# Batch 0's v in two halves around the token weights, its causal masks ahead of the scores, and batch 1's masks on GpSimd

## The chip, the cores and the metric

The kernel runs on one core of one Trainium2 chip. The metric is the device time of one execution in microseconds (us); the time before is the median of 5 runs. Engine names in the text: PE is TensorE (its weight loads, PEld, overlap it), DVE is VectorE, ACT is ScalarE, POOL is GpSimd, SP is SyncE, whose queue (SPq) issues the DMAs. L613 is line 613 of the kernel before.

## The reference

```
q, k, v: (8 batches, 8 heads, 576, 64)   s: (8, 8, 576)
scores = q @ k^T / 8;  cum = cumsum(max(s, 0))
scores = where(j > i, -1e9, scores + min(-(cum_i - cum_j), 0))
x = softmax(scores) @ v                  -> (8, 576, 512), the heads side by side
u = x + (relu(x^T @ w_tok1) @ w_tok2)^T  # w_tok1 576x256, w_tok2 256x576
out = u + relu(u @ w_ch1) @ w_ch2        # w_ch1 512x1536, w_ch2 1536x512
```

All inputs and the output are float32.

## The kernel before

Each batch goes through four stages. **Attention** works on four heads at a time (a "quad", heads 0 to 3 and 4 to 7). k and q of a quad come as one load each (L640), are cast to bf16 in two halves (L659 on POOL, L661 on DVE, L663 on ACT) and are rearranged by a DVE transpose (L670). The scores (L703) are computed in two phases, each into four PSUM banks of 128x512, keys on the partitions and a band of queries on the columns: only key blocks near the diagonal are kept. ACT takes their exponential into the tile E (L719). The decay of the reference is not added to the scores; it is put as a factor exp(cum_j − half) on row j of v and on a column of ones beside it, so the sum that divides comes out of the same product. The table wT of these factors comes from s (L567 to L586). Each 128-row chunk of v is loaded for all eight heads (L613, rows of 256 B) and multiplied by wT (L620) into the tile vp. The value product (L744, nine matmuls a head), a reciprocal (L753) and a normalisation (L758) give x.

The causal mask of the 128x128 diagonal blocks is made in one of two ways. In batches below PMASK, which is 2, TensorE adds it: after a phase's scores a matmul of the identity with the tile neg (0 or −30000) accumulates into the same banks (L712). In later batches POOL zeroes the upper triangle of E after the exponential (L727, one instruction for a key block of all four heads).

**Token mixing** multiplies x by w_tok1 and w_tok2. Batch 0 does it in four column blocks m so that it can begin with two heads (L864 first product, L871 relu, L877 transpose of x added in, L883 second product, L889 copy into uTa). Batch 1 and later do it for all columns (L969, L977, L994, L998), add x on DVE (L1011), and turn the result round by TensorE (L1024, L1032, batch 1) or by DMA. **Channel mixing** is L906 and L929 for batch 0 and L1052 and L1078 for the others. The weights are loaded in float32 into buffers that are used for other things later (uTb and x for the token weights, ga and vf for the channel weights), and cast to bf16 (L787 POOL, L789 DVE, L791 ACT). w_ch1 and w_ch2 come in four quarters each (L829, L837).

**The order is planned.** Each piece of work is put into a list with the engines that may run it, its costs on them, what it reads and writes, and a priority; `Plan.run` simulates the list several times, keeps the shortest plan, and the instructions are emitted in the order of the start times in it. Each engine then runs its own instructions in that order. The `lead` of an item is added to its urgency. The loads (`load_op`) are chained, so SP issues them in the order of the list. Rings of buffers (`Ring`, `Buf`) are handed out in the plan too; the PSUM rings are psc and pmx, four banks each. In the first 45 us of the plan, free PE time is filled with products of zeros (L1191). The loads of the start are listed as follows, which is the order of the SP queue:

```
stage_qk(0, 0); stage_s(); stage_qk(0, HQ); stage_v(0)
load_tok1; load_tok2; load_ch1 x4
stage_qk(1, 0); load_ch2(.., 0); stage_qk(1, HQ); load_ch2(.., 1); load_ch2(.., 2)
stage_v(1); load_ch2(.., 3); then batches 2 to 7
```

Of the kernel before, what the change touches and what calls it, by code (L numbers as in the profile page):

```python
# [49 lines left out]
class Plan:  # L50
# [101 lines left out]
    def run(self, passes=6):  # L152
# [3 lines left out]
        for i in range(passes):  # L156
            self.reset()
            if i >= 5:
                for o in self.ops:
                    o.tail = o.base + (rng.gauss(0.0, 2.0) if rng.random() < 0.1 else 0.0)  # L160
            order, length = self.once(i > 0)
            if best is None or length < best[0]:
                best = (length, [(o, o.start, o.fin, o.eng, o.fn) for o in order],
                        [(b, b.slot, b.begin, b.end) for o in order for b in o.bufs],
                        {r: list(r.uses) for o in order for b in o.bufs for r in (b.ring,)})
            self.lengths.append(round(length, 1))
            if i < 5 or best[0] == length:
                self.tails(order)
                for o in self.ops:
                    o.base = o.tail  # L170
# [9 lines left out]
    def once(self, use, eps=0.03):  # L180
# [14 lines left out]
        port = 0.0  # L195
        order = []

        def slot_time(o):
            t = 0.0
            want = {}  # L200
            for b in o.bufs:
                if b.slot is None:
                    r = b.ring
                    if b.ordered and r.queue[0] is not b:
# [237 lines left out]
def kernel(  # L442
# [28 lines left out]
    PMASK = 2  # L471
    HQ = 4
    TP = 128 // HQ
# [19 lines left out]
    neg = sb("neg", [128, 128], BF16, fast)  # L493
# [67 lines left out]
    def act(n, fn, bias=False):  # L561
# [3 lines left out]
        lambda: nc.sync.dma_start(out=s_sb[:, :], in_=s.rearrange("b h s -> (b h) s")), ["s"], 1.0)  # L565

    def decay():  # L567
        P.op(act(576, lambda: nc.scalar.activation(out=s_sb[:, :], in_=s_sb[:, :], func=AF.Relu)),
             reads=["s"], writes=["sr"], prio=-1)
        P.op({"DVE": (1.3, 1.6, lambda: nc.vector.tensor_tensor_scan(  # L570
            out=cum[:, :], data0=one_sb[:, :].to_broadcast([64, S]), data1=s_sb[:, :], initial=0.0, op0=ALU.mult, op1=ALU.add))},
            reads=["sr"], writes=["cum"], prio=-1)
        P.op(dve(1, lambda: nc.vector.tensor_scalar(
            out=half[:, :], in0=cum[:, S - 1 : S], scalar1=-0.5, scalar2=None, op0=ALU.mult)),
            reads=["cum"], writes=["half"], prio=-1)
        P.op(act(576, lambda: nc.scalar.activation(
            out=wn[:, 0:S], in_=cum[:, :], func=AF.Exp, bias=half[:, 0:1], scale=1.0), True),
            reads=["half", "cum"], writes=["wn"], prio=-1, lead=12.0)
        bw = Buf(r_sc, False)

        def w_tr():
# [6 lines left out]
            reads=[(bw, 0)], writes=["wT"], prio=-1)  # L588
# [11 lines left out]
    nc.vector.memset(ones[:, :], 1.0)  # L600

# [4 lines left out]
    def stage_v(b):  # L606
        vf, vp = Buf(r_vf), Buf(r_vp[b % 2])
        vbuf[b] = vp
        for c in range(NJ):
            n = min(128, S - c * 128)  # L610

            def load(c=c, n=n):
                nc.sync.dma_start(out=vf.t[0:n, c, :, :],  # L613
                                  in_=v[b, :, c * 128 : c * 128 + n, :].rearrange("h p d -> p h d"))
            load_op(load, [(vf, c)], 1.22 * n / 128)
        for c in range(NJ):
            n = min(128, S - c * 128)

            def mul(eng, c=c, n=n):
                eng.tensor_tensor(  # L620
# [619 lines left out]
```

## Time and profile before

| what | value |
|---|---|
| runs | 295.03 us median of 5 (294.57 to 297.26) |
| the profiled execution | 295.55 us, of which the span from first to last instruction is 293.7 us |
| PE busy | 279.3 us, 95% of the span |
| DVE, ACT, POOL busy | 171.5, 182.3, 93.5 us |
| DMA packets | 68050, 54.09 MB, mean 184 GB/s |
| L703 scores, L744 value product | 20.1 us and 18.4 us of PE |
| L712 masks by PE, both batches | 80 matmuls, from 9.6 to 48.2 us |
| L727 masks by POOL | 60 instructions, 36.1 us |

Busy time is how long an engine had an instruction in work; PE's ends are modelled, and the products of zeros count. A stage of the span is read by the engines' busy time in it, and what an engine waits for by the instruction that released it.

### The profile page before, as it was taken

How to read it: one execution, taken by the hardware profiler on the slowest of the kernel's cores; microseconds unless marked ns; L12 is line 12 of the kernel's file. 1: busy time of each engine (PE TensorE's matmuls, PEld its weight loads, DVE VectorE, ACT ScalarE, POOL GpSimd, SP SyncE). 2: the span in 40 equal slices, each digit the busy share in tenths (PEclk: the TensorE clock that was granted, in tenths of full speed). 3: DMA queues.
4: the chain of work that ended last, by engine and by line, in shares of the span. 5: the costliest groups of instructions: out<-in, count | busy, mean ns of one | idle time of the engine just before them, and what ended most of it. 6: DMA issues, size and time to landing. Idle time of an engine off the chain costs nothing.

```text
span 293.7 us, 6606 instructions
## 1 busy us (share of the span) xinstructions
PE 279.3 (95%) x2565; PEld 156.1 (53%) x2597; DVE 171.5 (58%) x332; ACT 182.3 (62%) x344; POOL 93.5 (32%) x138
## 2 busy tenths in 40 slices
PE   8899998969899989999999999999999999999994
PEld 2575455536664534546754545456754545347643
DVE  4883874987977625696847748596425523540022
ACT  3866865779897847965986178866882255007600
POOL 3443200858918412731481113821211210000000
PEclk9999999999999999999999999999999999999999
DMA  7999999998479999988493755567002420150023
GB/s 238 270 326 356 400 273 310 218 358 222 156 216 260 279 226 355 216 187 281 111 214 72 213 209 210 197 152 163 2 0 56 125 74 0 56 143 37 3 71 112
DMA packets 68050, 54.09 MB, mean 184 GB/s; under 512 B 53680, under 2 KB 56560, under 8 KB 68016
## 3 DMA queue, kind: packets, MB, share of 16 engines
q1 hardware_dynamic: 68016, 53.64, 64.8%
q8 instruction: 21, 0.34, 0.5%
q14 instruction: 13, 0.11, 0.1%
HBM read 40.65 MB, written 9.44 MB: 171 GB/s over the span
## 4 chain that ended last, share of the span: by engine, by line
PE 69%; DMA 12%; SPq 8%; DVE 4%; ACT 4%; issue 2%; POOL 1%; DVEq 0%; ACTq 0%
PE pmx L1052 27%; PE pmx L1078 22%; SPq L613 7%; DMA ga<-in_moe_w_ch_dram 4%; PE pmx L744 4%; PE psc L703 4%; PE pmx L994 4%; PE pmx L969 4%; DMA qkf<-in_q_dram 2%; DMA qkf<-in_k_dram 2%; DMA vf<-in_v_dram 2%; ACT E L719 1%; PE pmx L929 1%; ACT junk L645 1%; DMA uTa<-ua 1%
## 5 line engine op out<-in xcount | busy, mean ns | idle before, releaser
L719 ACT ACTIVATE E<-psc 128x512 bf16<-128x512 f32 x120 | 62.9, 603 | 20.9 <-PE psc L703 13.2
L1052 PEld LDWEIGHTS <-wc 128*128 128x128 bf16 x528 | 50.5, 98 | 35.5 <-issue 5.4
L727 POOL TENSOR_SCALAR_AFFINE_SELECT E<-E 128x512 bf16<-128x512 bf16 (+1 forms) x60 | 36.1, 631 | 86.9 <-ACT E L719 70.1
L1052 PE MATMUL pmx<-uTb,wc 128*128 128x320 bf16 x384 | 54.4, 299 | 2.5 <-ACT uTb L1032 1.7
L1078 PE MATMUL pmx<-wc,gb 128*128 128x512 bf16 (+1 forms) x245 | 53.2, 369 | 0.5 <-issue 0.2
L1058 ACT ACTIVATE gb<-pmx 128x320 bf16<-128x320 f32 x79 | 34.3, 439 | 24.3 <-PE pmx L1052 17.7
L645 ACT ACTIVATE junk<-qkf 128x1152 bf16<-128x1152 f32 x32 | 37.3, 1165 | 14.3 <-DMA qkf<-in_k_dram 9.4
L1078 PEld LDWEIGHTS <-gb 128*128 128x128 bf16 x252 | 23.8, 98 | 25.4 <-issue 0.7
L1052 PE MATMUL pmx<-uTa,wc 128*128 128x512 bf16 x137 | 32.4, 379 | 1.4 <-DMA uTa<-ua 1.0
L620 POOL TENSOR_TENSOR vp<-vf,wT 128x512 bf16<-128x512 f32 (+1 forms) x30 | 30.6, 1044 | 9.6 <-PE pmx L744 9.3
L1078 PE MATMUL pmx<-wc,ga 128*128 128x512 bf16 x138 | 32.6, 379 | 0.4 <-issue 0.2
L659 POOL CAST qkb<-qkf 128x1152 bf16<-128x1152 f32 (+1 forms) x15 | 15.7, 1045 | 38.4 <-DMA qkf<-in_q_dram 14.7
L758 DVE TENSOR_TENSOR x<-pmx,rc 128x320 bf16<-128x320 f32 x52 | 25.5, 490 | 1.7
L744 PEld LDWEIGHTS <-E 128*128 128x128 bf16 x576 | 20.9, 97 | 6.0 <-issue 0.9
L1058 ACT ACTIVATE ga<-pmx 128x512 bf16<-128x512 f32 x24 | 14.4, 599 | 15.0 <-PE pmx L1052 14.9
L670 DVE STREAM_TRANSPOSE kT<-qkb 128x576 f32<-128x576 f32 x16 | 20.1, 1255 | 5.7 <-PE psc L703 4.1
L1086 DVE TENSOR_TENSOR of<-pmx,ub 128x512 f32<-128x512 f32 (+1 forms) x17 | 11.2, 658 | 18.3 <-PE pmx L1078 14.5
L1078 PEld LDWEIGHTS <-ga 128*128 128x128 bf16 x144 | 13.3, 98 | 15.6 <-issue 1.1
L670 DVE STREAM_TRANSPOSE qT<-qkb 128x576 f32<-128x576 f32 x16 | 20.0, 1250 | 2.4 <-POOL qkb L659 1.1
L703 PE MATMUL psc<-qT,kT 32*128 32x256 bf16 (+2 forms) x592 | 20.1, 251 | 1.1 <-ACT E L719 0.4
L703 PEld LDWEIGHTS <-kT 32*128 32x128 bf16 x640 | 13.6, 92 | 11.3 <-issue 9.4
L744 PE MATMUL pmx<-vp,E 128*128 128x65 bf16 x468 | 18.4, 193 | 0.0
(107 smaller groups left out, 285.5 us busy)
## 6 DMA issues: line engine op xcount, KB each, us to landing
qkf<-in_k_dram SPq DMA_DIRECT2D x20, 576.0 KB, 6.0
qkf<-in_q_dram SPq DMA_DIRECT2D x20, 576.0 KB, 6.1
vf<-in_v_dram SPq DMA_DIRECT2D x32, 256.0 KB, 6.0
out_dram<-of SPq DMA_DIRECT2D x31, 256.0 KB, 2.6
ga<-in_moe_w_ch_dram SPq DMA_DIRECT2D x6, 768.0 KB, 7.5
vf<-in_moe_w_ch_dram SPq DMA_DIRECT2D x2, 768.0 KB, 9.8
out_dram<-of SPq DMA_DIRECT2D x10, 128.0 KB, 2.7
vf<-in_v_dram SPq DMA_DIRECT2D x8, 128.0 KB, 5.2
```

The lines of the kernel that those rows point to most:

```text
L613: nc.sync.dma_start(out=vf.t[0:n, c, :, :], in_=v[b, :, c * 128 : c * 128 + n, :].rearrange("h p d -> p h d"))
L620: eng.tensor_tensor(out=vp.t[0:n, c, :, 0:D], in0=vf.t[0:n, c, :, :], in1=wT[0:n, c, b * H : b * H + H].unsqueeze(2).to_broadcast([n, H, D ...
L645: P.op({"ACT": (1.1, 1.5, lambda: nc.scalar.activation(out=junk[:, :], in_=f.t[:, :], func=AF.Square, accum_out=sq[:, col : col + 1]))}, r ...
L670: nc.vector.transpose(out=T.t[:, 0:S, :].rearrange("p s q -> p (s q)").bitcast(FP32).rearrange("p (t r) -> p r t", r=R), in_=t1.t[:, :].bi ...
L703: nc.tensor.matmul(out=ps[e].t[:, c0 : c0 + z - a], lhsT=kT.t[p0 : p0 + TP, jc * 128 : jc * 128 + 128, qq], rhs=qT.t[p0 : p0 + TP, a:z, qq ...
L719: nc.scalar.activation(out=E.t[:, e, ph * 512 : ph * 512 + 512], in_=p.t[:, :], func=AF.Exp, scale=0.125)
L727: nc.gpsimd.affine_select(out=w, in_=w, compare_op=ALU.is_ge, fill=0.0, base=0, pattern=[[0, HQ], [1, n]], channel_multiplier=-1)
L744: nc.tensor.matmul(out=o[:, ic, 0 : D + 1], lhsT=E.t[:, hh, d0 : d0 + 128], rhs=vp.t[:, jc, h + hh, 0 : D + 1], start=(jc == j_lo), stop=( ...
L758: nc.vector.tensor_tensor(out=x.t[:, :, (h + hh) * D : (h + hh + 1) * D], in0=o[:, :, 0:D], in1=rc.t[:, :].unsqueeze(2).to_broadcast([128, ...
L1052: nc.tensor.matmul(out=pm.t[:, 0 : e - a], lhsT=wc1[:, m, cc * 128 : cc * 128 + 128], rhs=uT.t[:, m, a:e], start=(m == 0), stop=(m == NMC ...
L1058: lambda cc=cc, pm=pm, a=a, e=e: nc.scalar.activation(out=g.t[:, cc, a:e], in_=pm.t[:, 0 : e - a], func=AF.Relu),
L1078: nc.tensor.matmul(out=pm.t[:, na:nb], lhsT=g.t[:, cc, c * 128 : c * 128 + 128], rhs=wc2[:, cc, na:nb], start=(cc == 0), stop=(cc == NCC - 1))
```

## The change

- v of batch 0 is loaded and scaled in two parts of four heads. The first part stays where v was; the second is listed behind both token weights, with the second quad behind it. Of the first part's five chunks the first three (c up to VP = 2) are scaled by POOL only; the rest of batch 0's may go to POOL or DVE.
- PMASK goes from 2 to 1: batch 1 is masked by POOL on E.
- In batch 0 the mask product comes ahead of the scores of its phase, as an item of its own that needs only the tile neg. neg is now 256 wide, the right half zero, so the mask product writes the whole width of each key block and opens the accumulation; the scores close it.
- The casts of batch 0's k and q have a fixed engine each. The token weights' casts may go to POOL or ACT (only POOL before), and w_tok2 is cast in two pieces.
- The list of loads has k and q of batch 1's second quad ahead of the first quarter of w_ch2.
- Planner: batch 0's items get large leads; costs of some loads differ; batch 0's score and value banks are handed out in a listed order; `run` does 5 plain passes and 60 more with small random changes of urgency around the best so far (one such pass before).

The diff, cut to its core:

```diff
-    def run(self, passes=6):
+    def run(self, passes=5, search=60):
...
-            if i >= 5:
+            if i >= passes:
                 for o in self.ops:
-                    o.tail = o.base + (rng.gauss(0.0, 2.0) if rng.random() < 0.1 else 0.0)
+                    o.tail = base[o] + (rng.gauss(0.0, 2.0) if rng.random() < 0.02 else 0.0)
...
-    PMASK = 2
+    PMASK = 1
     HQ = 4
+    VP = 2
...
-    neg = sb("neg", [128, 128], BF16, fast)
+    neg = sb("neg", [128, 256], BF16, fast)
...
+    nc.vector.memset(neg[:, 128:256], 0.0)
...
-    def stage_v(b):
+    def stage_v(b, part=None):
...
+        parts = [(0, HQ), (HQ, H)][part : part + 1] if b == 0 else [(0, H)]
+        for (h0, h1) in parts:
+            for c in range(NJ):
+                n = min(128, S - c * 128)
+
+                def load(eng, c=c, n=n, h0=h0, h1=h1):
+                    eng.dma_start(out=vf.t[0:n, c, h0:h1, :],
+                                  in_=v[b, h0:h1, c * 128 : c * 128 + n, :].rearrange("h p d -> p h d"))
+                load_op(lambda load=load: load(nc.sync), [(vf, c, h0)], 1.25 * n / 128 * (h1 - h0) / H + (0.5 if b == 0 and c == NJ - 1 else 0.0))
...
+                w = (h1 - h0) * D
+                alts = {"POOL": (*c_pool(w, 0.0019), lambda mul=mul: mul(nc.gpsimd))}
+                if b == 1 or b == 0 and (h0 or c > VP):
+                    alts["DVE"] = (*c_dve(w), lambda mul=mul: mul(nc.vector))
...
+                if b == 0:
+                    one = (("DVE", "ACT"), ("ACT", "POOL"), ("POOL", "POOL"), ("POOL", "POOL"))[2 * (h // HQ) + i][hf]
+                    alts = {one: alts[one]}
...
+            def mask(ps=ps, cols=cols):
+                for e in range(HQ):
+                    for (jc, a, z, c0) in cols:
+                        nc.tensor.matmul(out=ps[e].t[:, c0 : c0 + z - a], lhsT=ident[:, :], rhs=neg[:, 0 : z - a],
+                                         start=(c0 == 0), stop=False)
+            mocc = HQ * 512 / 2400.0 + 0.05
+            if pem:
+                P.op({"PE": (mocc, mocc + 0.3, mask)}, reads=["neg"], writes=[(p, 1) for p in ps], prio=(np_, 0))
...
-                if pem:
-                    for e in range(HQ):
-                        for (jc, a, z, c0) in cols:
-                            n = min(128, S - jc * 128)
-                            nc.tensor.matmul(out=ps[e].t[:, c0 : c0 + n], lhsT=ident[:, :], rhs=neg[:, 0:n],
-                                             start=False, stop=(jc == cols[-1][0]))
...
     stage_qk(0, HQ)
-    stage_v(0)
-    for h in range(0, H, HQ):
-        quad(0, h)
-    av0 = lastav[0]
+    stage_v(0, 0)
+    quad(0, 0)
     load_tok1(Buf(r_uTb))
     load_tok2(Buf(r_x))
+    stage_v(0, 1)
+    quad(0, HQ)
...
+    av0 = lastav[0]
...
     stage_qk(1, 0)
+    stage_qk(1, HQ)
     load_ch2(sga, 1536, 0)
-    stage_qk(1, HQ)
     load_ch2(sv, 0, 1)
```

## The prediction

> **What bounds the kernel now.** I read four views in this order: the stages (busy time of each engine between two times), TensorE's timeline, SyncE's timeline with each load's time to landing, and TensorE's waits.
>
> Stages. The columns are span, then busy time of PE, PEld, DVE, ACT, POOL, then clock, DMA share and GB/s:
>
> ```profile
> 10.50:12.00 1.50, 1.23 (x37) 1.06 (x25) 1.42 (x2) 1.50 (x4) 0.71 (x2) 1.00 1.31 217
> 18.00:19.50 1.50, 1.50 (x45) 1.38 (x44) 1.32 (x7) 0.78 (x2) 0.88 (x2) 1.00 1.04 377
> ...
> 36.00:51.00 15.00, 14.55 (x188) 9.05 (x189) 8.79 (x12) 9.37 (x19) 0.67 (x1) 1.00 1.01 293
> 57.00:67.00 10.00, 6.99 (x82) 3.76 (x82) 8.30 (x14) 6.67 (x13) 6.60 (x9) 1.00 1.03 338
> ```
>
> The DMA engines are full in all four, but the bytes differ: v travels at 217 GB/s, the token weights at 377. From 36 to 51 TensorE is nearly full too, and GpSimd does 0.67 us of work in 15. From 57 to 67 TensorE has 3 us of holes. After 67 it is full again nearly to the end (44.25 of 45 us from 165 to 210), so what is won before about 66 us reaches the end of the kernel whole.
>
> TensorE, in time (start, length, line, output<-inputs, idle before and its releaser):
>
> ```profile
> 17.86 1.02 PE L744 MATMUL psc<-vp,E 128*128 128x65 bf16 x28 [0.64 <-DVE vp L620]
> 20.12 1.03 PE L864 MATMUL psc<-x,w 128*128 128x128 bf16 x10
> 26.92 8.58 PE L906 MATMUL pmx<-uTa,wc 128*128 128x512 bf16 x38
> ...
> 35.99 0.62 PE L712 MATMUL psc<-neg,ident 128*128 128x128 bf16 x8
> 51.40 0.81 PE L929 MATMUL pmx<-wc,gb 128*128 128x512 bf16 x3 [0.63 <-DVE wc L789]
> 56.17 1.89 PE L969 MATMUL pmx<-x,w 128*128 128x512 bf16 x8
> 66.47 3.96 PE L1052 MATMUL pmx<-uTb,wc 128*128 128x320 bf16 x28 [1.74 <-ACT uTb L1032]
> ```
>
> Until 26 us TensorE is fed by arrivals: the value product waits for the last scaled chunk of v, and batch 0's token mixing (L864, four columns m) then runs as a latency chain until L906 starts. The second limit is at 51.40: L929 waits for the last quarter of the second channel weight, cast as it lands. SyncE's queue shows why both come late:
>
> ```profile
> 3.57 8.94 SPq L613 DMA_DIRECT2D vf<-in_v_dram  x5
> 12.55 0.62 SPq L800 DMA_DIRECT2D uTb<-in_moe_w_tok_dram  x1
> 13.77 1.53 SPq L812 DMA_DIRECT2D x<-in_moe_w_tok_dram  x1
> ...
> 43.30 0.57 SPq L837 DMA_DIRECT2D ga<-in_moe_w_ch_dram  x1
> ```
>
> Adding each issue's time to landing: the last q lands at 10.5, v's last chunk at 11.35+5.75 = 17.1, the first token weight at 18.9, the second at 20.2, the first quarter of w_ch1 at 22.3, batch 1's v at 46.3, the last quarter of w_ch2 at 43.30+7.06 = 50.4.
>
> **What the Trainium skill says.** "DMA: Bandwidth & Descriptors", Specifications: transfers under 512 B do not reach line rate. v moves in 256 B rows, in halves as well as whole; 217 against 377 GB/s agrees, so halving v cheapens no byte. "TensorE: Matmul & The Clock Gate", Part 3, The mechanism: matmuls start and end strictly in program order. The trace agrees: while the 28 value matmuls wait 0.64 us nothing else of TensorE runs. So what is queued behind a late half of v waits too. "GPSIMD Engine Reference", Key points: GpSimd shares its SBUF interfaces with VectorE, and they contend. The trace agrees: one GpSimd cast of 128x576 took 1.57 us among others of 0.66.
>
> **The change, part by part.**
>
> *Loads.* v occupied the queue for 17.1 − 10.5 = 6.6 us, so a half takes 3.3. First half complete 13.8; token weights 3.3 us earlier, at 15.6 and 16.9; second half 16.9+3.3 = 20.2, which is 3.1 later than now; w_ch1 unchanged at 22.3, since the bytes ahead of it are the same. SyncE gets five more issues, about 0.5 us each (an unstalled v issue took 0.48): 2.5 us. Cover: SyncE afterwards sits 5.5 us waiting for the cast of w_ch1. Without that cover the fourth quarter of w_ch1 would be up to 2.5 us late. I take 0.
>
> *Scaling v.* Now five VectorE products of about 0.68 us, beginning at 13.85 when the decay table wT is there. After: GpSimd must take three half chunks. Its 128x512 product takes 1044 ns, so a half is about 0.52 (up to 1.2 if it contends like the 1.57 cast); VectorE's half is 0.34. From 13.8: 13.8 + 3×0.52 = 15.4 (VectorE does the other two alongside). The first four heads' value products then run 15.4 to 16.5 (four times 0.27) where they now end at 18.9.
>
> *Token mixing of batch 0.* The first weight's casts (1.5 us on GpSimd) move from 18.62 to about 15.6, done 17.1, so L864 of m=0 starts near 17.1 instead of 20.12; m=1 follows. m=2 and 3 wait for the second half of v: 20.2 + 0.5 scaling = 20.7, value products from there, then four reciprocal-and-normalise pairs of 0.18+0.45 on VectorE: done about 23.5. L864 of m=3 at 23.5 against 24.64 now; with 0.9 for it, 0.38, 0.43 and 0.42 for relu, product and copy, uTa is complete at 25.6 to 26.0 against 28.0. L906's first group (12 matmuls of 0.216) can do its nine m=0..2 pieces inside that chain, leaving three: it ends near 26.7 against 29.2. **TensorE is ahead by 2.5.** The next quarter of w_ch1 is cast by 25.9 and doesn't stop it.
>
> *Masks of batch 0 ahead of the scores.* They widen from 128 to up to 256 columns: 4×512 columns at L906's pace of 512 in 0.216 us, 0.86 us a phase instead of about 0.5, +1.4 us in four phases. Cover: TensorE fills this stretch with dummy matmuls (1.04 us at 12.13) and waits for qT. If uncovered, scores are 1.4 us late. In return each phase's first exp loses a wait of about 0.5. Bounds −0.5 to +1.4; I take 0, because the exps end (14.9 for the first four heads) ahead of v.
>
> *Masks of batch 1 to GpSimd.* Removed from TensorE: four groups, 0.46+0.79+0.46+0.58 us from their start to the next matmul: **2.3 us**. Added: ten selects, about 8×0.63+2×0.41 = 5.9 us on GpSimd, in the stretch where it has 0.67 of 15 busy. Behind them stand its casts of k and q of batch 2, from 51.98. The value product now waits for the selects; scaled v of batch 1 is there only at 47.1, so they cost 0 unless the exps stay as late as now (50.2), then +1.7 (three selects).
>
> *w_ch2's first quarter behind two more q/k loads.* 1.18 MB at 405 GB/s = 2.9 us: lands 36.9, cast 37.9. L929 begins now at 38.18, so of the 4.8 us ahead most turns into waiting there. The last quarter still lands at 50.4 (same bytes ahead). The gain returns only as other work done earlier: with batch 1's masks and scores out of the way, the value products can follow v at 47.1 and VectorE's eight normalisations (4.3 us now, from 51.25) end near 52. At 51.4 just L929's last 12 matmuls are left, 2.6 us: L969 at 54.0 against 56.17, **−2.2**. Putting a few of those into the 0.2+0.9+1.7 us of holes between L994 and L1052 gives up to 2 more; I count 0.3.
>
> *New planner costs, leads and 60 noisy passes* cost no instruction, but change the static order everywhere. Unknown, −1.5 to +2 (the holes before 67 can be filled, or as many made); I take 0.
>
> Sum: −2.5 on the profiled execution: span 293.7 to 291.2, time 295.55 to 293.05. That execution is 0.5 above the median of 295.03, so the median goes to **292.5**.
>
> **Rivals.** (a) *The order also fills the token-mixing holes of batch 1.* For: 3.0 us of holes in 57 to 67 and w_ch2's last matmuls free to go there; against: they hold all four pmx banks. −5: 290.0, chance 0.22. (b) *The late weight swallows it*: value products stay behind L929's wait, L969 moves only by the masks after 51.4, −1: 294.0, chance 0.13. For: 50.4 is unmoved; against: v is there 4 us earlier. (c) *The second half of v becomes the wait.* Its 256 B rows share the DMA engines with w_ch1's quarters issued behind it. If it lands with the second of them at 24.4, uTa ends 24.4 − 20.2 later than 25.8, at 30.0 against 28.0, and strict order holds L906 behind it; with a reordered remainder that recovers nothing, +2: 297.0. It decides from a landing of about 22.5 on, where uTa is no earlier than now. Against: v's loads mostly landed in issue order. Chance 0.15. (d) That the early half buys nothing (the planner places the work otherwise) ends like (b) and is counted there.
>
> **Numbers.** Forecast case 0.50, its own range 291 to 294. The measurement tells 0.5% (1.5 us) from no change. Faster: 0.22 + nearly all of 0.50 = 0.70; same: (b) and the forecast's edge, 0.15; slower 0.15. The range 289.0 to 297.0 takes in (a) and most of (c).
>
> **What would show it.** Right: L864 starts near 17, L906 by about 24 and its first group ends near 26.7; no L712 after 20 us; GpSimd selects between 36 and 47; L969 near 54; L1052 near 64. Wrong: a TensorE wait on vp or x above 1.5 us at 20 to 24, the last w_ch2 cast later than 51.5, or L969 at 56 or later.

## The result, and the profile after

The changed kernel takes 296.45 us (median of 42 runs) beside 295.39 us for the kernel before (79 runs): ratio 1.0032, 95% interval 1.0015 to 1.0049. By that ratio it is 0.9 us slower; the ratio leaves out executions that fell into a second, slower state, so it is a little below the quotient of the two medians. The forecast was 2.5 us faster. The profiled execution after took 295.28 us with a span of 293.5 us. Line numbers have moved: the mask product L712 is now L721, the scores L703 are L732, the value product L744 is L770, token mixing L864 is L890, the first channel products L906 and L929 are L932 and L955, then L969 is L995 and L1052 is L1078; the loads of v are L622, those of the channel weights L855 and L863, their cast on ACT L817.

The stages of the profile after, columns as in the prediction:

```profile
9.00:10.50 1.50, 1.50 (x32) 1.26 (x35) 1.21 (x2) 0.47 (x1) 1.48 (x2) 0.50 1.19 296
18.00:19.50 1.50, 1.45 (x27) 0.98 (x25) 1.27 (x6) 1.50 (x5) 1.31 (x3) 1.00 0.77 143
...
36.00:51.00 15.00, 14.84 (x157) 7.59 (x158) 10.45 (x14) 10.02 (x20) 8.53 (x12) 1.00 1.07 309
57.00:67.00 10.00, 9.31 (x100) 5.22 (x99) 9.07 (x15) 8.82 (x17) 8.06 (x11) 1.00 1.00 318
```

Three things are to be seen. The granted clock is 0.50 at 9 us (it was full throughout before). The DMA engines are no longer full at 18 us (share 0.77 against 1.04, 143 against 377 GB/s), nor from 27 to 30 (241 GB/s against 419). GpSimd's busy time from 36 to 51 rose from 0.67 to 8.53, and the 3 us of holes in 57 to 67 shrank to 0.7: the masks moved and the holes were filled, as was hoped, and yet the kernel isn't faster.

TensorE in time, after:

```profile
8.99 1.04 PE L732 MATMUL psc<-qT,kT 32*128 32x256 bf16 x16 [3.38 <-DVE qT L688]
17.45 1.26 PE L770 MATMUL psc<-vp,E 128*128 128x65 bf16 x36
19.82 1.03 PE L890 MATMUL psc<-x,w 128*128 128x128 bf16 x10 [0.24 <-DVE x L784]
23.09 1.25 PE L770 MATMUL pmx<-vp,E 128*128 128x65 bf16 x36
...
28.73 8.37 PE L932 MATMUL pmx<-uTa,wc 128*128 128x512 bf16 x37
53.15 0.81 PE L955 MATMUL pmx<-wc,gb 128*128 128x512 bf16 x3 [1.24 <-ACT wc L817]
56.83 1.89 PE L995 MATMUL pmx<-x,w 128*128 128x512 bf16 x8
64.40 1.26 PE L1078 MATMUL pmx<-uTb,wc 128*128 128x320 bf16 x8 [0.57 <-DVE uTb L1060]
```

The last masks of the first quad end at 5.6, then TensorE waits 3.38 us for qT. The value product starts at 17.45, only 0.4 ahead of before, although its half of v is scaled at 15.1; L890 starts at 19.82 (20.12 before). The second quad's value product comes at 23.09, behind two columns of token mixing, and the channel product's long run starts at 28.73, where it was 26.92. L955 then waits 1.24 us for the last cast of w_ch2, and L995 is 0.7 us later than before. L1078 starts 2.1 us ahead of before's 66.47, and yet the span is only 0.2 shorter (293.5 against 293.7): that lead does not last. The end of the point-by-point section comes back to it.

SyncE's queue, after:

```profile
12.14 5.78 SPq L622 DMA_DIRECT2D vf<-in_v_dram  x5
17.96 1.79 SPq L855 DMA_DIRECT2D ga<-in_moe_w_ch_dram  x2
25.75 0.37 SPq L855 DMA_DIRECT2D ga<-in_moe_w_ch_dram  x1
45.76 0.58 SPq L863 DMA_DIRECT2D ga<-in_moe_w_ch_dram  x1
```

Issue to landing added, the first half of v is complete at 13.6, the token weights at 15.1 and 18.1, the second half of v at 20.6, the first quarter of w_ch1 at 23.3, the last of w_ch2 at 51.6. The fourth quarter of w_ch1 (25.75) was issued at 23.57 before, because its buffer is free only when the first quarter is cast. ACT's queue, first before, then after, shows why that cast is late:

```profile
22.72 0.82 ACT L791 CAST wc<-ga 128x768 bf16<-128x768 f32 x1
```

```profile
23.82 1.15 ACT L790 ACTIVATE x<-pmx,rc 128x64 bf16<-128x64 f32 x5
24.81 0.88 ACT L817 CAST wc<-ga 128x768 bf16<-128x768 f32 x1
```

ACT's half of the first quarter stands behind a normalisation of batch 0 (L790) that comes from the second half of v. It ran at 22.72 before; of the 2.1 us, about 1.0 is the later landing (23.3 instead of 22.3). Every later load is issued behind it. The last quarter of w_ch2 lands at 51.6 instead of 50.4, and its cast is on ACT (1.47 us) and no longer on VectorE (0.96), so it ends at 53.10 instead of 51.34.

### The profile page after: what moved, and what is told of

It is laid out like the page before. It is cut to its first block, busy times and chain, and to the rows that moved or that the text cites. A ratio compares the mean times of both kernels' runs of the same rounds, so it can differ in the third digit from the quotient of the medians.

```text
span 293.5 us, 6512 instructions
## 1 busy us (share of the span) xinstructions
PE 276.7 (94%) x2511; PEld 155.0 (53%) x2542; DVE 171.5 (58%) x330; ACT 182.7 (62%) x350; POOL 103.5 (35%) x155
## 4 chain that ended last, share of the span: by engine, by line
PE 66%; DMA 14%; DVE 7%; SPq 4%; ACT 3%; POOL 2%; issue 2%; ACTq 0%; POOLq 0%; DVEq 0%
PE pmx L1104 24%; PE pmx L1078 23%; DMA vf<-in_v_dram 5%; DMA qkf<-in_q_dram 5%; PE psc L732 4%; PE pmx L770 4%; SPq L622 3%; PE pmx L995 3%; PE pmx L1020 3%; DMA ga<-in_moe_w_ch_dram 2%; DMA qkf<-in_k_dram 2%; ACT E L743 2%; DVE qT L688 1%; PE psc L890 1%; DVE kT L688 1%
## 5 line engine op out<-in xcount | busy, mean ns | idle before, releaser
L751 POOL TENSOR_SCALAR_AFFINE_SELECT E<-E 128x512 bf16<-128x512 bf16 (+1 forms) x70 | 43.0, 642 | 96.0 <-ACT E L743 74.1
L743 ACT ACTIVATE E<-psc 128x512 bf16<-128x512 f32 x120 | 63.3, 602 | 21.1 <-PE psc L732 20.2
L1078 PEld LDWEIGHTS <-wc 128*128 128x128 bf16 x528 | 50.6, 98 | 34.2 <-issue 1.9
L1078 PE MATMUL pmx<-uTb,wc 128*128 128x320 bf16 x384 | 54.2, 299 | 1.1 <-DVE uTb L1060 0.6
L1084 ACT ACTIVATE gb<-pmx 128x320 bf16<-128x320 f32 x84 | 36.0, 437 | 23.9 <-PE pmx L1078 18.1
L630 POOL TENSOR_TENSOR vp<-vf,wT 128x512 bf16<-128x512 f32 (+2 forms) x35 | 34.9, 1017 | 11.9 <-PE pmx L770 9.4
L1078 PE MATMUL pmx<-uTa,wc 128*128 128x512 bf16 x138 | 32.3, 379 | 1.2 <-DVE of L1112 0.8
L784 DVE TENSOR_TENSOR x<-pmx,rc 128x320 bf16<-128x320 f32 x51 | 23.9, 486 | 1.2
L732 PE MATMUL psc<-qT,kT 32*128 32x256 bf16 (+2 forms) x592 | 20.2, 255 | 4.0 <-DVE qT L688 3.4
L770 PEld LDWEIGHTS <-E 128*128 128x128 bf16 x576 | 20.6, 97 | 6.0 <-issue 1.7
L673 POOL CAST qkb<-qkf 128x576 bf16<-128x576 f32 (+1 forms) x16 | 15.2, 957 | 21.7 <-DMA qkf<-in_q_dram 11.6
L1112 DVE TENSOR_TENSOR of<-pmx,ub 128x512 f32<-128x512 f32 (+1 forms) x17 | 11.2, 658 | 18.4 <-PE pmx L1104 16.5
L732 PEld LDWEIGHTS <-kT 32*128 32x128 bf16 x640 | 14.1, 95 | 13.6 <-issue 10.0
L770 PE MATMUL pmx<-vp,E 128*128 128x65 bf16 x468 | 18.2, 193 | 0.8 <-DVE gb L1086 0.7
```

The lines of the kernel that those rows point to most:

```text
L630: eng.tensor_tensor(out=vp.t[0:n, c, h0:h1, 0:D], in0=vf.t[0:n, c, h0:h1, :], in1=wT[0:n, c, b * H + h0 : b * H + h1].unsqueeze(2).to_broa ...
L673: nc.gpsimd.tensor_copy(out=o.t[:, a:z], in_=i.t[:, a:z])
L732: nc.tensor.matmul(out=ps[e].t[:, c0 : c0 + z - a], lhsT=kT.t[p0 : p0 + TP, jc * 128 : jc * 128 + 128, qq], rhs=qT.t[p0 : p0 + TP, a:z, qq ...
L743: nc.scalar.activation(out=E.t[:, e, ph * 512 : ph * 512 + 512], in_=p.t[:, :], func=AF.Exp, scale=0.125)
L751: nc.gpsimd.affine_select(out=w, in_=w, compare_op=ALU.is_ge, fill=0.0, base=0, pattern=[[0, HQ], [1, n]], channel_multiplier=-1)
L770: nc.tensor.matmul(out=o[:, ic, 0 : D + 1], lhsT=E.t[:, hh, d0 : d0 + 128], rhs=vp.t[:, jc, h + hh, 0 : D + 1], start=(jc == j_lo), stop=( ...
```

## The experiments

My theory after this reading: (1) the early masks hold all eight PSUM banks, so nothing can fill TensorE from 5.6 to 9.0, its clock falls, and the head starts late; (2) the split of v delays the end of token mixing by the order of the queues, and the cast of w_ch1 with it; (3) the loads decide until about 66 us, so the 2.3 us of mask work taken from TensorE is worth nothing. Rivals: the masks on GpSimd cost by themselves, or the planner's new static order does it all. Ratios are to the kernel before, with 95% intervals.

**The clock.** Seven products of zeros are accumulated into the first quad's mask banks, right behind its masks; the plan is the same.

```
+ if first quad's last masks:
+     for i in range(7): matmul(out=ps[i % 4], lhsT=zero, rhs=zero, start=False, stop=False)
```

> The changed kernel with seven 128x512 products of zeros accumulated into banks of the first quad right behind its early masks; order and everything else the same. In the changed kernel the masks hold all eight PSUM banks from 2.8 us, TensorE is idle from 5.6 to 9.0 and the granted clock is 0.5 from about 8.3 to 15.1. Theory 'cold start': the clock stays at 1.0, the second quad's first scores start near 14.0 instead of 15.3, the first value product near 16 instead of 17.45, and 0.5 to 1.5 us of it reach the end (about 295 on the scale where the changed kernel is 296.4). Rival 'second half of v': the scaling of the second half still ends near 21.5 and the token mixing follows it as a chain, so uTa is complete within 0.3 us of 29.8 and the end within 0.4 us of the changed kernel's.

Measured 1.0014 (0.9986 to 1.0042). TensorE's timeline of this kernel:

```profile
8.89 0.64 PE L735 MATMUL psc<-qT,kT 32*128 32x256 bf16 x16 [1.44 <-DVE qT L688]
...
16.53 1.24 PE L773 MATMUL psc<-vp,E 128*128 128x65 bf16 x36 [0.48 <-DVE vp L642]
...
53.52 0.81 PE L958 MATMUL pmx<-wc,gb 128*128 128x512 bf16 x3 [2.27 <-ACT wc L820]
```

With the clock kept full, 16 score matmuls take 0.64 instead of 1.04 us, and the value product and what follows come 0.9 us earlier (16.53 against 17.45, the long channel run 27.79 against 28.73). At the last cast of w_ch2 the gain is gone: the wait grew by 1.0, from 1.24 to 2.27. The clock is a real cost of the head. At the end the two versions stand at 1.0032 and 1.0014, which is 0.5 us apart, the low edge of what the theory gave; the intervals overlap, so what the clock costs the whole kernel isn't settled.

The counterpart is the kernel before with its zero products of 5.3 to 8.9 us left out:

```
- fills.append(f)
+ if not 5.3 < t0 < 8.9: fills.append(f)
```

> The kernel before without the products of zeros that its plan puts between 5.3 and 8.9 us; order the same. Theory 'cold start': the clock falls to 0.5 for about 7 us from 8 to 9 us on, scores and masks of both quads take up to twice their time, the second quad's exponentials end near 20 instead of 18.8, and the end is 0.5 to 1.5 us later. Rival: v's last chunk lands at 17.1 anyway, the value product starts within 0.3 us of 17.86, and the end stays within 0.4 us.

Measured 1.0000 (0.9977 to 1.0023). TensorE's timeline:

```profile
8.86 0.92 PE L703 MATMUL psc<-qT,kT 32*128 32x256 bf16 x16 [3.90 <-DVE qT L670]
...
17.07 1.25 PE L744 MATMUL psc<-vp,E 128*128 128x65 bf16 x36
```

The first quad's scores and masks are about as slow as after the change, and the value product isn't late. But the half clock lasted only 3.4 us here (9.0 to 12.5), not the 7 expected and not the 6.8 of the changed kernel. In the order of before this much of it costs nothing. That the early half of v is what took its cover away is argued, not tested.

**The parts alone.** The new planner loop in the kernel before:

```
- def run(self, passes=6):
+ def run(self, passes=5, search=60):    # and the changed loop
```

> The kernel before with the changed kernel's planner loop alone (5 plain passes and 60 with small random changes of urgency). No instruction is added; the order differs everywhere. Theory 'the order is a lottery of about 1 us': between 1 us faster and 1 us slower, with holes of TensorE moved among the stages between 50 and 90 us. Rival 'the search finds real time': 1 to 2 us faster, by fewer holes between 57 and 67.

Measured 1.0001 (0.9977 to 1.0025). And PMASK = 1 alone in the kernel before, with its own six passes:

```
- PMASK = 2
+ PMASK = 1
```

> The kernel before with batch 1 masked by GpSimd (PMASK 1) and nothing else. Theory 'wait for the last weight': TensorE loses 2.3 us of mask products between 36 and 49 but waits that much longer for the last quarter of w_ch2 at about 51.4, so the end moves by less than 0.7 us. Rival 'TensorE is the bound': 1.5 to 2.3 us faster. Rival 'selects are late': the value products of batch 1 wait for GpSimd behind the exponentials, 1 us or more slower.

Measured 1.0068 (1.0041 to 1.0095): taking 2.3 us of matmuls off TensorE made the kernel 2.0 us slower. The theory allowed 0.7, and the size is that of the rival in which the selects come late; but no value product waits for GpSimd in the profile. Its TensorE:

```profile
51.48 1.46 PE L929 MATMUL pmx<-wc,gb 128*128 128x512 bf16 x6 [1.76 <-ACT wc L791]
56.02 1.90 PE L969 MATMUL pmx<-x,w 128*128 128x512 bf16 x8 [0.71 <-DVE x L758]
```

The freed time came back as a longer wait for the same cast (1.76 against 0.63 before), then two new ones. L969 starts at 56.02, against 56.17. This execution took 294.06 us, 2.5 below the median of its kernel, so what made the kernel slower isn't seen in it.

**Is that wait the wall?** The last group of batch 0's second channel product reads the first quarter of w_ch2 instead of the last, so it need not wait. The edit was made in the warm version of the changed kernel, in the kernel before, and in the kernel before with PMASK = 1.

```
- rhs=wc2[:, cc, :]
+ rhs=wc2[:, cc % (NCC - CG), :]
```

> The warmed changed kernel (ratio 1.0014), in which batch 0's last group of channel products reads the first quarter of w_ch2 in place of the last; all loads, casts and the order are the same, only TensorE's wait for the last quarter is left out. Theory 'late last weight': the wait of 2.27 us before 53.52 goes, the products after it move forward by about that, and 1.5 to 2.3 us reach the end: ratio 0.994 to 0.997. Rival 'the next chain takes it': the normalised x of batch 1 or later loads then wait instead, L995's stage moves by less than 0.7 us and the end stays within 0.5 us of the warmed kernel's.

> The kernel before with the same edit: batch 0's last group of channel products reads the first quarter of w_ch2, so its wait of 0.63 us at 51.40 is left out. Both theories: 0 to 0.6 us faster, ratio 0.998 to 1.000. It is the yardstick for the other two.

> The kernel before with batch 1 masked by GpSimd (ratio 1.0068), and the same edit. Its wait of 1.76 us before 51.48 is left out. Theory 'late last weight': 1 to 1.8 us faster than with the wait, ratio 1.000 to 1.003. Rival 'the next chain takes it': the wait of L969 for x grows from 0.71 to over 2 us and the ratio stays above 1.004.

Measured 1.0037 (1.0003 to 1.0072), 0.9992 (0.9959 to 1.0025) and 1.0046 (1.0015 to 1.0078). The wait goes, the time stays; the third ratio is what its rival gave. ACT in the first of them:

```profile
62.80 1.15 ACT L677 CAST qkb<-qkf 128x1152 bf16<-128x1152 f32 x1 [1.29 <-DMA qkf<-in_k_dram]
...
64.35 0.58 ACT L1061 COPY uTb<-pmx 128x512 bf16<-128x512 bf16 x1
```

The copy of uTb, for which the next channel product waits 1.26 us, stands in ACT's queue behind the cast of a k that has just landed. So one wait taken out brings nothing: in this profile the next load holds the engine that TensorE needs. That a sequence of loads decides, and not something else in the order, this suggests and doesn't show.

**The loads.** If loads decide, cheaper loads must pay. First batch 0's v alone, in the changed kernel, in rows of 1 KB instead of 256 B, which are other rows of v.

```
- in_=v[b, h0:h1, c * 128 : c * 128 + n, :].rearrange("h p d -> p h d")
+ in_=v[b, c if h0 == 0 else c + 3, 0 : 4 * n, :].rearrange("(p r) d -> p (r d)", r=4)
```

> The changed kernel with batch 0's v read in rows of 1 KB instead of 256 B (as many bytes into the same places, from other addresses of v, so batch 0's values are those of other rows); order the same. Theory 'v's rows stall the queue': SyncE no longer stalls in the second half's issues, the first quarter of w_ch1 lands at 21 or earlier instead of 23.3 and its fourth quarter is issued 1 to 2 us earlier, the last quarter of w_ch2 is cast by about 52 instead of 53.1, and the end is 0.7 to 1.5 us earlier than the changed kernel's. Rival: the chain behind w_ch1's casts is set by ACT and by buffers, the last quarter lands within 0.5 us of 51.6, and the end moves by less than 0.4 us.

Measured 1.0011 (0.9986 to 1.0037). Its stages:

```profile
24.00:25.50 1.50, 1.50 (x25) 0.89 (x21) 1.34 (x6) 1.50 (x7) 0.96 (x3) 1.00 0.01 3
25.50:27.00 1.50, 1.50 (x18) 1.02 (x16) 0.40 (x2) 0.74 (x2) 1.50 (x2) 1.00 0.02 8
```

The columns end with DMA share and GB/s. The second half of v had landed at 17.5, the first quarter of w_ch1 was issued at 13.80 instead of 17.96, and then the DMA engines stood still for 3 us: the fourth quarter was issued at 25.92, as late as ever, since the cast ahead of it waits behind the normalisation on ACT. VectorE scaled the second half only from 20.65 to 22.36, behind the first quad's normalisations, and its value product stayed at 23.25, the channel run at 28.90. So neither the bytes nor the issues of v's second half set the head's end; the order on VectorE, TensorE and ACT does. The last quarter of w_ch2 still landed at 51.7, as the rival had it.

Then v of batches 0 to 2 in rows of 2 KB (1 KB for the halves of the changed kernel's batch 0), in both kernels:

```
- in_=v[b, :, c * 128 : c * 128 + n, :].rearrange("h p d -> p h d")
+ in_=v[b].rearrange("h (x r) d -> (h x) (r d)", r=8)[c * 128 : c * 128 + n, :]     # b <= 2
```

> The kernel before with v of batches 0, 1 and 2 read in rows of 2 KB instead of 256 B (as many bytes into the same places, from other addresses of v, so these batches' values are those of other rows); order the same. Theory 'the loads decide until about 66 us': each v takes some 2.5 us less, the last quarter of w_ch2 lands near 46 instead of 50.4, L1052 starts 1.5 us or more earlier, and the end is 1.5 to 4 us earlier (ratio 0.986 to 0.995). Rival 'TensorE's fixed order decides': only the waits of 0.6 us at 17.9 and 0.6 us at 51.4 go, ratio 0.996 to 1.000.

> The changed kernel with the same edit (rows of 1 KB for the halves of batch 0's v, 2 KB for batches 1 and 2); order the same. If the loads decide, TensorE's 2.3 us of masks saved in batch 1 now count: ratio at or below that of the kernel before with long rows, although the fourth quarter of w_ch1 is still issued near 25.8 (it waits for a cast on ACT). If the change's own order is what costs, it stays 0.002 to 0.006 above that ratio.

Measured 0.9950 (0.9925 to 0.9975) and 0.9966 (0.9938 to 0.9995): the first at the edge of what the theory gave, the second 0.0016 above it, between its two cases. TensorE of the first, then of the second:

```profile
26.44 8.58 PE L910 MATMUL pmx<-uTa,wc 128*128 128x512 bf16 x39
...
63.41 2.89 PE L1056 MATMUL pmx<-uTb,wc 128*128 128x320 bf16 x20
```

```profile
28.73 8.37 PE L937 MATMUL pmx<-uTa,wc 128*128 128x512 bf16 x38
...
63.31 1.26 PE L1083 MATMUL pmx<-uTb,wc 128*128 128x320 bf16 x8 [0.57 <-DVE uTb L1065]
```

No wait for a weight is left in either. The changed kernel starts its channel run 2.3 us later and is level at 63.3: the masks on GpSimd earn their 2.3 us there and pay for the head. They do so without cheaper loads too. From the start of the channel run to L1078 the changed kernel went from 28.73 to 64.40; the kernel before without its early zeros went from 26.36 to 64.60. That is 2.6 us made up; the warm version, which started at 27.79 and came to 64.77, made up 1.3. So part (3) of the theory, that the masks' time is worth nothing, fits PMASK = 1 alone in its first order (no gain) and not the changed kernel, where by these profiles it is spent on the late head.

**The cast.** ACT's half of the first quarter's cast is put ahead of its normalisations of batch 0 (in the warm version):

```
+ for o in first:          # ACT's half of the cast of w_ch1's first quarter
+     o.start = min(o.start, nr - 0.001)    # nr: first ACT normalisation
```

> The warmed changed kernel (1.0014) with ACT's half of the cast of w_ch1's first quarter moved ahead of ACT's normalisation of batch 0; nothing else. Theory 'the cast holds the queue': the fourth quarter of w_ch1 is issued near 24 instead of 25, later loads land about 1 us earlier, the last quarter of w_ch2 is cast about 1 us earlier and the wait of 2.3 us before it shrinks as much; 0.5 to 1 us of it reach the end, ratio 0.998 to 1.000. Rival: the normalisation, now 0.8 us later, delays the token mixing by as much and the end is the same or later.

Measured 1.0031 (1.0003 to 1.0060). The fourth quarter was issued at 24.90, no earlier than in the warm version (24.82), because the first quarter itself landed 0.9 us later in this execution. Yet the last quarter of w_ch2 landed at 50.2 instead of 52.0 and the wait for it was gone: that landing doesn't follow from the fourth quarter's issue alone. The third column of token mixing waited 0.68 us for ACT's normalisation and the channel run went from 27.79 to 29.28. As the rival had it, the end is no earlier. Filling the DMA gap instead, with batch 1's first k and q ahead of w_ch1's fourth quarter (kernel before, PMASK = 1, noisy passes):

```
+ stage_qk(1, 0)
  load_ch1(sga, 0, 3)
- stage_qk(1, 0)
```

> The kernel before with three edits: k and q of batch 1's first quad are listed ahead of w_ch1's fourth quarter (which has to wait for a buffer), so the queue has work while that waits; batch 1 masked by GpSimd; the planner's 60 noisy passes. Theory 'the loads decide': the DMA engines lose no time at 24 to 27 us (283 to 295 GB/s in the kernel before), later loads land about 1 us earlier, and the masks' 2.3 us begin to count: ratio 0.993 to 0.998. Rival: w_ch1's fourth quarter comes too late for L906 and the order elsewhere is a lottery: 0.999 to 1.005.

Measured 1.0016 (0.9979 to 1.0053). From 24 to 27 us the DMA engines moved 402 GB/s, but the wait for the last cast of w_ch2 was still 1.51 us.

**Parts of the change taken back, and other orders of the same program.** What was open by then was the share of v's split, of the masks, of the moved first quarter of w_ch2, and of the planner's luck. In the changed kernel: v whole again, both halves (still ten issues) ahead of the first quad; PMASK back at 2; the first quarter of w_ch2 ahead of the second quad's k and q again; and only another random seed.

```
a_vwhole:  stage_v(0, 0); + stage_v(0, 1); quad(0, 0); ...; - stage_v(0, 1); quad(0, HQ)
a_pm2:     - PMASK = 1          + PMASK = 2
a_chfirst: stage_qk(1, 0); load_ch2(sga, 1536, 0); stage_qk(1, HQ)
a_seed5:   - random.Random(1)   + random.Random(5)
```

> The changed kernel, but batch 0's v is loaded and scaled whole again, ahead of the first quad and of both token weights; masks ahead of scores and all of batch 1's masks on GpSimd stay. Theory (splitting v is what delays token mixing, by the order of TensorE's queue and by the cast that stands behind it): the first channel product starts near 27 as before the change (28.73 with the split), the fourth quarter of w_ch1 is issued near 23.6 (25.75 with the split), the last w_ch2 lands near 50.4 instead of 51.6; ratio to the kernel before 0.998 to 1.001. Rival (the planner's order elsewhere is what costs the rest, the split nothing): ratio 1.002 to 1.005 with the early times as told. Second rival (the masks ahead of scores hold PSUM and are the cost): first channel product at 28 or later even with v whole.

> The changed kernel, but GpSimd takes every second mask of the wide pair only as before (PMASK = 2), so that batch 1's other masks are on TensorE again, about 2.3 us of it between 36 and 51. Theory (the loads decide until 66 us, so TensorE's time there is free): the same time as the changed kernel within 0.2%, the wait for the last w_ch2 cast shrinks by what the masks take. Rival (the masks' 2.3 us reach the end): 0.7% slower than the changed kernel, that is 1.010 to the kernel before.

> The changed kernel, but the first quarter of w_ch2 is loaded ahead of the second quad's q and k of batch 1, as before the change. Theory (the last quarter's landing decides, and the bytes ahead of it are the same): within 0.2% of the changed kernel, last w_ch2 lands at 51 to 52. Rival (the moved quarter is what is late): 0.4% or more faster than the changed kernel.

> The changed kernel with another random seed for the planner's noisy passes: the same instructions, another static order. Theory that +0.3% is partly the luck of one order: the ratio to the kernel before differs from 1.003 by 0.2% or more in either direction, while the first channel product still starts at 28 to 29.5 and TensorE still waits for the last w_ch2 cast. Rival (the cost lies in the operations and loads): 1.003 within 0.1%.

Measured 1.0135 (1.0088 to 1.0181), 1.0220 (1.0170 to 1.0271), 1.0128 (1.0070 to 1.0185) and 1.0023 (0.9998 to 1.0048). The first three miss the numbers of every theory. The other seed is within 0.1% of the changed kernel, as its rival had it, although TensorE doesn't wait for the last cast of w_ch2 in it. TensorE's timelines show where the three lost their time. With v whole:

```profile
27.84 9.01 PE L932 MATMUL pmx<-uTa,wc 128*128 128x512 bf16 x40
...
81.50 1.79 PE L1078 MATMUL pmx<-uTb,wc 128*128 128x320 bf16 x12 [2.22 <-DVE gb L1086]
```

The head gains 0.9 of the 1.8 us, L1078 starts at 64.5 as in the changed kernel, and then come a new hole of 2.22 us at 79 and one of 1.07 at 90. With the moved quarter put back, the last quarter of w_ch2 lands at 53.0, TensorE waits twice as long for its cast, and L1078 starts 3.4 us later than in the changed kernel. A second long wait follows:

```profile
54.05 2.29 PE L955 MATMUL pmx<-wc,gb 128*128 128x512 bf16 x5 [2.48 <-DVE wc L815]
67.84 4.05 PE L1078 MATMUL pmx<-uTb,wc 128*128 128x320 bf16 x28
...
96.63 0.38 PE L1020 MATMUL pmx<-h,w 128*128 128x512 bf16 x1 [2.65 <-DVE ua L1037]
```

With PMASK = 2 TensorE does all masks of batch 1 again (the expectation tells this edit wrongly), and in the new form, up to 256 columns wide and ahead of the scores; so it doesn't restore the masks of before. The plan was another from the first matmuls on: the second quad's scores at 18.15, L995 at 61.50. So a single edit, replanned, is no clean experiment here. Two more runs kept the edit and changed only the planner's passes: v whole with another seed, and PMASK = 1 in the kernel before with the 60 noisy passes.

```
a_vwhole_s2: a_vwhole, - random.Random(1) + random.Random(2)
b_pm1s:      - PMASK = 2 + PMASK = 1, and run(self, passes=5, search=60)
```

> The changed kernel with batch 0's v whole again, as in the run before, but with another random seed for the noisy passes: the same instructions in another static order. Theory (the 1.35% that the first order with whole v cost are holes of that order between 76 and 94 us, 2.2 and 1.1 us of waits of TensorE, not the price of whole v): ratio to the kernel before below 1.008, first channel product at 27 to 28. Rival (whole v together with the early masks costs 1%): 1.010 or more again.

> The kernel before with two parts of the change alone: all masks of batch 1 on GpSimd and the planner of the change with its 60 noisy passes. Theory (until 66 us the loads decide, so the masks bring nothing; the +0.7% of the same edit without the noisy passes was holes of one order): 0.998 to 1.004. Rival (the masks' 2.3 us count once the order is a good one): 0.994 or less, which would be a version that beats both.

Measured 1.0050 (1.0023 to 1.0078) and 1.0157 (1.0109 to 1.0206). By the ratios two orders of the same instructions with v whole differ by 0.85%. The profiles don't bear that out: the spans are 295.6 and 295.5 us, and the other order has the same two waits, 1.07 us at 90 and

```profile
81.76 1.79 PE L1078 MATMUL pmx<-uTb,wc 128*128 128x320 bf16 x12 [1.53 <-DVE gb L1086]
```

So the theory that the 1.35% were holes of one order isn't shown, though its ratio came; the first ratio rests on 6 runs, the second on 22. Either way v ahead of the first quad shows no gain. The second run missed both expectations for a reason of its own, which its timelines of TensorE, VectorE and GpSimd show together:

```profile
82.80 3.46 PE L1055 MATMUL pmx<-uTb,wc 128*128 128x320 bf16 x15 [4.77 <-DVE gb L1063]
```

```profile
75.92 6.44 DVE L1142 TENSOR_TENSOR_SCAN s_sb<-one_sb,wn 64x576 f32<-64x576 f32 x1
```

```profile
76.22 1.21 POOL L730 TENSOR_SCALAR_AFFINE_SELECT E<-E 128x512 bf16<-128x512 bf16 x2
77.39 2.23 POOL L662 CAST qkb<-qkf 128x1152 bf16<-128x1152 f32 x2
79.58 1.58 POOL L730 TENSOR_SCALAR_AFFINE_SELECT E<-E 128x256 bf16<-128x256 bf16 x3
```

A scan of VectorE, of the same shape as one that takes 1.28 us at the start of the kernel, took 6.44 us here, beside an unbroken run of GpSimd instructions, and TensorE waited 4.77 us for a copy queued behind it. That is 1.6% of the span, all of what the run lost. Less that, it would stand level with the kernel before, as the theory that the masks bring nothing had it; that subtraction is an argument and not a run. It also cuts the other way. The run with k and q ahead of w_ch1's fourth quarter (1.0016) has the same stall:

```profile
76.31 5.15 DVE L1142 TENSOR_TENSOR_SCAN s_sb<-one_sb,wn 64x576 f32<-64x576 f32 x1
```

TensorE waited 2.77 us behind it. Less that, that run would stand 0.8% ahead of the kernel before, about where its theory had it: masks on GpSimd and a filled DMA gap together may be worth something that this order hid. No run settles it.

## Why the prediction was wrong, step by step

Two steps failed. The first is the head: instead of 2.5 us ahead, TensorE came to its first channel product 1.8 us behind (28.73 against 26.92), of which the half clock is 0.9, and the rest is the order, in which other work stands ahead of the value products. The second is that what is won before 66 us should reach the end whole: the lead of 2.1 us at L1078 became 0.2. Where the last 0.3% come from is open.

- **Loads: mostly right, in part by luck.** First half of v, token weights and second half landed at 13.6, 15.1 to 18.1 and 20.6, against 13.8, 15.6 to 16.9 and 20.2. "SyncE gets five more issues … I take 0" named its cover. The ten issues of v took 12.5 us against 8.9 for five, 3.5 more and not 2.5, and w_ch1's first quarter came at 23.3 instead of 22.3. The fourth quarter was 2.2 us late, within the "up to 2.5" without cover; but the cast held it (the 1 KB run) and not the issues, so that agreement is luck.
- **Scaling v: right in the sum.** 15.1 against 15.4. VectorE's two half chunks took 0.65 us each and not 0.34, but it and GpSimd began early enough.
- **"Masks of batch 0 ahead of the scores … I take 0, cover: dummy matmuls": failed.** The cover was destroyed by the step itself. The masks take all eight PSUM banks from 2.8 and 4.4 us on, long before any score (8.99), so no product of zeros has a bank. The clock was at half from 8.1 to 14.9. The second quad's scores began at 15.32 instead of 13.54, 1.8 later, past the bound of +1.4; with the clock kept full they began at 13.86. Warming it gives 0.9 us at the value product.
- **"The first four heads' value products then run 15.4 to 16.5", "L864 of m=0 starts near 17.1": failed.** They began at 17.45 and 19.82. Of the value product's 2.0 us, 0.9 is the clock; the rest is that the second quad's masks and scores stand ahead of the value product (12 masks at 15.89 and 24 score matmuls at 16.88 run directly before it). I had moved the value product to where its data was ready and not asked what the order puts before it.
- **"uTa is complete at 25.6 to 26.0 … TensorE is ahead by 2.5": failed, and this is the main term of the head.** uTa was complete at 29.8. The second half of v was scaled at 21.6, close to the 20.7 assumed; its value product ran at 23.09, behind two columns of token mixing, and the 1 KB run, with v landed sooner, left it at 23.25. TensorE was 1.8 behind at L932, not 2.5 ahead: 4.3 us of error.
- **"w_ch1 unchanged", "the last quarter still lands at 50.4": failed, by a queue that I did not price.** ACT's half of the cast was put behind its normalisations of the late half. 2.2 us later issue, DMA engines at 0.66 to 0.77 of their time around it, last landing 51.6, last cast to 53.1. How much of the last landing is due to that issue is open: with the fourth quarter issued at 24.8 and 24.9 it came at 52.0 and 50.2. The prediction's own sign of error, "the last w_ch2 cast later than 51.5", is the one that came, and so did "L969 at 56 or later".
- **Batch 1's masks: size right, value wrong.** No mask product after 20 us, ten more selects (43.0 us in 70 of them, against 36.1 in 60), 2.3 us off TensorE. "L969 at 54.0, −2.2" came at 56.83: the lead ahead of the masks was missing, and TensorE waited 1.24 us at L955 for the last cast. By L1078 TensorE had made up what the head had lost against the kernel before without early zeros (64.60), and no more.
- **"What is won before about 66 us reaches the end of the kernel whole": failed in the pair of profiles.** "L1052 near 64", a sign of being right, came: L1078 starts at 64.40, 2.1 ahead of 66.47. But the span is only 0.2 shorter. At 170 us, at the same point of the work, 1.2 us of the lead were left (170.23 against 171.42). The span was expected to take over all that stood at 66 us, and it took over about a tenth.
- **"New planner costs … unknown, −1.5 to +2; I take 0": the bounds were too narrow.** Orders of one program differed by 0.1% (the other seed) and by 0.9% (PMASK = 1 alone, 1.0068 and 1.0157), and replanned edits lay 0.2 to 2.2% above the kernel before.
- **The rivals.** (c) gave the right sign and too large a size, +2 against 0.9, by the wrong mechanism: the late half landed at 20.6 and not after 22.5; what was late was its place in the queues. (b), the late weight swallows the gain, describes 50 us rightly, except that there was no gain left to swallow. (a) failed: the holes of 57 to 67 were filled, L1078 came forward by 2.1 us against the profile of before, and the end did not.

One part is open: where the last 0.3% come from. The warm version (1.0014) and the kernel without early zeros (1.0000) start batch 1's first channel product at 64.8 and 64.6 us: level. (The 66.47 in the profile of before, with its wait of 1.74, is that one execution's.) They are still level at 170 us, where by the records 940 matmuls are left in both. First the kernel without early zeros, then the warm one:

```profile
169.86 2.76 PE L1052 MATMUL pmx<-uTa,wc 128*128 128x512 bf16 x12
172.56 0.64 PE L703 MATMUL psc<-qT,kT 32*128 32x256 bf16 x24
...
199.03 1.25 PE L1052 MATMUL pmx<-uTb,wc 128*128 128x320 bf16 x8
```

```profile
169.70 2.76 PE L1081 MATMUL pmx<-uTa,wc 128*128 128x512 bf16 x12
172.39 0.57 PE L735 MATMUL psc<-qT,kT 32*128 32x256 bf16 x2
173.18 0.27 PE L735 MATMUL psc<-qT,kT 32*128 32x256 bf16 x1 [0.22 <-ACT E L746]
173.67 0.61 PE L735 MATMUL psc<-qT,kT 32*128 32x256 bf16 x21 [0.22 <-ACT E L746]
...
200.97 0.71 PE L1081 MATMUL pmx<-uTb,wc 128*128 128x320 bf16 x4
```

At the last line the warm version is 1.9 us later and has done one more group of scores (0.6 us), so it lost 1.5 us from 170 on, as much as its span is longer (293.0 against 291.5). Of these, 1.25 are one group of 24 scores that waits for exponentials and takes 1.82 us instead of 0.57. The exponentials stand on ACT behind a sum over a k that landed at 170.3 instead of 169.2. So in this pair the head and the masks together cost the end nothing, and most of the difference is one wait at 172 us. But the same group took 1.54 us in the profile of before and 2.00 in that of the changed kernel. The wait is thus not the change's own, and its size varies with the execution. Whether the last 0.3% is this wait, this order's luck or what is left of the head, these runs don't settle. No version tried that computes the same beats both kernels.

## What to carry to other kernels

Work taken off the busiest engine can come back as waiting, as it did with PMASK = 1 alone (0.63 us became 1.76): first ask which transfer the next wait ends on. A lead at one point of the kernel is not yet a lead at its end: find the same point of the work later on in both profiles and compare again. Moving an operation earlier is not free because its engine idles there; ask which buffers it then holds, and what used to fill that time. When an order is planned anew with every edit, run the same edit with two or three orders before a difference of 1% is put down to the edit: PMASK = 1 alone measured 1.0068 in one order and 1.0157 in another.

## What the runs showed of the hardware

- TensorE was idle from 5.6 to 9.0 us in the changed kernel and its clock at half from 8.1 to 14.9; 16 score matmuls took 1.04 instead of 0.64 us. In the kernel before without early zeros it was idle from 5.0 to 8.9 and at half from 9.0 to 12.5. Seven zero products in between, leaving a wait of 1.44, kept the clock full. The Trainium skill, "TensorE: Matmul & The Clock Gate", What's actually happening, puts the fall to half rate after an idle window of about 3.4 us; the stretches at half rate, 6.8 and 3.4 us, fit windows of that length, but the first fall came already 2.5 us after the last mask product.
- The second half of v in 256 B rows held SyncE's queue for 5.78 us: four issues of 0.47 to 0.55 us and a last one of 3.57. In 1 KB rows the five took 2.40 us, none over 0.47. So small rows cost the issuing queue too, and not only bandwidth.
- VectorE's second scan (64x576) took 1.28 to 2.15 us in all profiles but two: 5.15 us and 6.44 us. In both it lay beside an unbroken run of GpSimd instructions and ended 1.2 us after the last of them (80.26 to 81.46, 81.16 to 82.36), just under its own duration. That it was shut out until then is what this suggests: the scan reads two SBUF tensors, and the Trainium skill, "GPSIMD Engine Reference", Key points, names just such VectorE instructions as contending with GpSimd. It gives no size, and no run tested it by itself.
